# Two-layer spectral mixer and MLP on one core: third pair's sums on VectorE, half-width products around the last norm, matrix loads over 15 steps, more places for second weights

## The chip, the core and the metric

The kernel runs on one core of a Trainium2 chip. The engines are named as in the profile: PE (TensorE, with its weight loads as PEld), DVE (VectorE), ACT (ScalarE), POOL (GpSimd) and SP (SyncE), which here issues the program's DMA transfers. The metric is device time of one execution in microseconds (us), and of several executions the median.

## The reference

Four residual sublayers on x of shape (1, 2048, 576), all in float32: Fourier mixing, MLP, Fourier mixing, MLP. The MLP's weights are the same in both layers.

```python
def _A_ref(x, ...):                      # Fourier mixing
    a = einsum("bsd,ed->bse", x, dft_hid_re)
    b = einsum("bsd,ed->bse", x, dft_hid_im)
    return einsum("ts,bse->bte", dft_seq_re, a) - einsum("ts,bse->bte", dft_seq_im, b)

def _B_ref(x, w1, b1, w2, b2):           # w1: 576 x 4608, w2: 4608 x 576
    y = _layernorm(x, axis=-1)
    h = gelu(einsum("bsd,df->bsf", y, w1) + b1)
    return einsum("bsf,fd->bsd", h, w2) + b2

x = x + _A_ref(_layernorm(x)); x = x + _B_ref(_layernorm(x))
x = x + _A_ref(_layernorm(x)); x = x + _B_ref(_layernorm(x))
```

## The kernel before

**Number format.** A matmul operand is kept as two float32r parts, the rounded value (high) and the remainder (low). ACT writes the high part and DVE or POOL subtracts it to get the low one. A product is then three passes: high by high, high by low, low by high (`PASSES`).

**Seven products.** The big products are cut into 2 by 2 blocks and done with seven block products in place of eight; sums and differences of blocks are made before, and PE's results are combined by DVE, ACT and POOL after. `ORDER` is the order of the seven (1, 6, 2, 5, 7, 3, 4), `BANK` the PSUM bank of each: 1 and 2 share bank 0, 6 has bank 1, 5 and 3 share bank 2, 7 and 4 share bank 3. So product 2 can only start when product 1 has been copied out, 3 after 5 has been read, 4 after 7.

**Stages of a layer.** First the product along the sequence (`Sequence`). Then, for each half of the 2048 rows (first half, second half), eight row tiles of the product along the hidden dimension with the second layer norm (`hidden`), and the MLP on that half (`mlp`). The MLP goes over nine rounds `g`, each with two `inner` products (first weights, 512 columns) and the `outer` products of the round before (second weights): first the products 1, 6, 5, 3 (`OUTER[0]`), and after the second `inner` 7, 4, 2 (`OUTER[1]`). Each outer product is two steps of 12 matmuls, and the last round's outer products are 14 steps.

**What sets the order.** The program is a straight list; each engine runs its instructions in the order in which the Python code issues them, and waits on semaphores for data and for buffers. All DMA transfers stand in SP's one queue, in program order, so that a transfer that waits holds up the transfers behind it. Memory is two heaps, R (float32r) and A, in which places are taken and given back in program order.

**A tile end.** This happens four times, at the end of `hidden` (first and second layer, first and second half). The eight tiles make four pairs j = 0 to 3. For a pair, four blocks of the normalized rows are transposed (`turn_blocks`), then `turn_sums` writes the split of three of the blocks (`parts`, L846 on ACT and L194 on DVE) and makes four differences of 128 x 384 in place, and `turn_parts` writes the split of those four. For the last pair (j = 3) four differences of 128 x 288 are made on DVE in `norms` before the transposes, and `turn_y` transposes and splits its seven blocks in six pieces. The MLP's first product set is done in two halves: part 0 (256 columns, pairs 0 and 1) is a generator that yields after each of its seven products, and is advanced by `next(mlp)` here between the transposes; part 1 (pairs 2 and 3) follows and needs everything that `turn_parts(2)` and `turn_y(3)` write. Before the change the third pair (j = 2) has its differences on POOL during the last tile, and its parts, the last norm (L241) and the four differences of the last pair all come before the first copy (L1081) of the MLP's product 1.

**A hand-over.** This happens once a layer, from the MLP of the first half to `hidden` of the second half. During the last round's 14 outer steps `outer` advances a second generator, `steps()`, which loads the nine hidden matrices (R<-dh_parts, 576 KB each), the rows of the sequence product (R<-uv_mid) and x, and transposes the first tile. The matrices go to the place of `Y`, the MLP's input, which is given back at `g == NG`, when the last `inner` is over. Meanwhile the second weights of the last products need places too (`c2`): two from the start, and a third at `EXTRA_AT`. In the second layer `load_w` reads the prepared second weights (R<-w_parts) into a free place; in the first layer `make` prepares them (`hi` on ACT at L998, `lo` on DVE at L194), writes them out (w_parts<-R), and takes a place for each.

Of the kernel before, what the change touches and what calls it, by code (L numbers as in the profile page):

```python
# [153 lines left out]
def spectral_mixer(ctx: ExitStack, tc: tile.TileContext, x, dh, c0, cs, w1, b1, w2, b2, out):  # L154
# [487 lines left out]
    class Hidden:  # L642
# [42 lines left out]
        def steps(self):  # L685
            self.uvs = Slots(R, 2, 2 * D, Y_AT[0])
            self.X = A.place(X_AT[1], NT * DH)
            self.places = [R.place(Y_AT[0] + 4 * D + k * 2 * D, 2 * D) for k in range(KH)]

            def load_d(k):  # L690
                b = self.places[k].at
                self.load_d(k, Block(R, b, D), Block(R, b + D, D))

            self.load(0)
            load_d(0)
            yield
            self.load(1)
            load_d(1)
            for k in range(KH):
                yield  # L700
                if k + 2 < KH:
                    load_d(k + 2)
                self.high_d(k)
                if k:
                    self.low_d(k - 1)
            yield
            self.low_d(KH - 1)
            drain(self.turn(0, R.place(UT_AT[1][0], 2 * KH * P)))
            self.load_uv(2)
            yield  # L710
# [66 lines left out]
    def hidden(h, mlp):  # L777
# [18 lines left out]
        def norms(n):  # L796
# [10 lines left out]
            if n < NP - 1:  # L807
                add(nc.gpsimd, tile_x, tile_x, b2t(2, DH))
            else:
                b12, b22, b11, b21 = (v[:, k] for k in range(4))  # L810
                t1, t3, t2, t4 = (v[:, k] for k in range(4, 8))
                sub(nc.vector, t1, b12, b11)
                sub(nc.vector, t3, b22, b12)
                sub(nc.vector, t2, b22, t1)
                sub(nc.vector, t4, b21, t2)
# [34 lines left out]
        def turn_sums(j):  # L850
# [4 lines left out]
            g = nc.gpsimd  # L855
# [38 lines left out]
        for n in range(NP):  # L894
# [16 lines left out]
            for k in range(KH):  # L911
                if n == 0 and k == KH // 2:
                    drain(turn(1))
                if n >= 3 and n % 2 and k == 2:
                    turn_sums((n - 3) // 2)
# [11 lines left out]
            if n >= 3 and n % 2:  # L927
                turn_parts((n - 3) // 2)
            if n >= 2 and n % 2 == 0:
                turn_blocks(n // 2 - 1)  # L930


        drain(*ln)
        rests(3)
        y_steps = turn_y(3)
        for n in range(7):
            next(mlp)
            for _ in range((0, 0, 0, 1, 2, 1, 2)[n]):
                next(y_steps)
# [12 lines left out]
    def mlp(hid, store, first, after):  # L952
# [186 lines left out]
        def outer(g, i, side):  # L1139
            for jj in range(2):  # L1140
# [17 lines left out]
                if g == last:  # L1158
# [27 lines left out]
        for g in range(NG + 1):  # L1186
# [3 lines left out]
            if g == NG:  # L1190
                work(99)
                c1.close()
                hs.close()
                Y.free()
            for f in range(2):
                if g < NG:
                    for _ in inner(2 * g + f, None if g or f else 1):
                        pass
                if g:
# [86 lines left out]
```

## Time and profile before

| what | value |
|---|---|
| runs, us | 2773.51, 2768.78, 2773.53; median 2773.51 |
| profiled execution, us | 2768.23 |
| its span, first to last instruction, us | 2766.4 |
| granted PE clock, mean over the span | 0.992 |
| PE busy, us (share) | 2675.7 (97%) |
| DVE, ACT, POOL busy, us (share) | 1763.8 (64%), 1104.0 (40%), 804.9 (29%) |
| DMA, mean rate | 197 GB/s |

A row of the timeline reads: start in us, length in us, engine, line of the kernel, operation, what is written and read, shapes, count of merged instructions, and in square brackets the engine's idle time before it with what ended it. In a row of the windows stand the stretch, its length, the busy time of the engine with its count, the granted PE clock (1.00 is full speed), the busy share of the DMA engines and their GB/s.

### The profile page before, as it was taken

What the parts mean: (1) busy time and instruction counts of PE and PEld (TensorE: products, weight loads), DVE (VectorE), ACT (ScalarE), POOL (GpSimd) and SP (SyncE); (2) the same over time, 40 slices, a digit from 0 to 9 for tenths busy, and PEclk for the clock granted to TensorE, in tenths of its full rate; (3) what the DMA queues carried; (4) which work ended last, traced back from release to release, by engine and by line L of the source; (5) the groups of instructions that cost most, each with busy time, mean ns of one, the idle gap of its engine ahead of it and who ended that gap; (6) DMA issues with size and microseconds to landing.
All of it is one profiled execution on the core that took longest, in us unless ns stands there. A gap on an engine that the chain in (4) does not pass through costs nothing.

```text
span 2766.4 us, 45317 instructions
## 1 busy us (share of the span) xinstructions
PE 2675.7 (97%) x17488; PEld 2507.4 (91%) x17488; DVE 1763.8 (64%) x2566; ACT 1104.0 (40%) x1838; POOL 804.9 (29%) x762
## 2 busy tenths in 40 slices
PE   7999999999999999999989999999999999999998
PEld 7999998788888988989889999998999989898988
DVE  8788866777776465555577666555555545655555
ACT  6555545544443343333344333344333313433331
POOL 5222224544534432222251000042222224221222
PEclk9999999999999999999999999999999999999999
DMA  5666675777775646566553333526666563566664
GB/s 199 238 225 221 230 261 172 266 265 271 264 265 211 221 152 195 192 196 192 167 208 119 123 120 129 191 99 208 193 195 192 190 251 129 186 194 197 192 196 151
DMA packets 208711, 543.73 MB, mean 197 GB/s; under 512 B 21985, under 2 KB 56801, under 8 KB 208353
## 3 DMA queue, kind: packets, MB, share of 16 engines
q1 hardware_dynamic: 208496, 540.84, 57.8%
q8 instruction: 138, 2.26, 0.3%
q14 instruction: 77, 0.62, 0.1%
HBM read 428.69 MB, written 114.72 MB: 196 GB/s over the span
## 4 chain that ended last, share of the span: by engine, by line
PE 81%; DVE 6%; DMA 4%; issue 4%; POOL 2%; ACT 2%; SPq 0%; POOLq 0%; ACTq 0%; DVEq 0%
PE bank L201 80%; DVE R L194 3%; DMA R<-w_parts 2%; POOL A L194 2%; PE bank L764 1%; DVE A L191 1%; DMA A<-x_mid 1%; DMA A<-in_w 1%; DVE A L194 0%; DVE moments L231 0%; DVE bank L191 0%; DMA w_parts<-R 0%; ACT A L241 0%; SPq L188 0%; POOL R L194 0%
## 5 line engine op out<-in xcount | busy, mean ns | idle before, releaser
L201 PE MATMUL bank<-R 128*128 128x288 f32 (+2 forms) x16972 | 2629.7, 316 | 83.4 <-DVE A L191 26.3
L201 PEld LDWEIGHTS bank<-R 128*128 128x128 f32 x16972 | 2451.9, 190 | 250.5 <-DVE A L191 32.6
L191 DVE TENSOR_TENSOR A<-bank,A 128x576 f32<-128x576 f32 (+3 forms) x808 | 566.9, 710 | 565.2 <-PE bank L201 484.0
L194 POOL TENSOR_TENSOR R<-A,R 128x512 fp32r<-128x512 f32 x288 | 374.8, 1312 | 978.8 <-ACT R L1114 955.7
L194 DVE TENSOR_TENSOR R<-A,R 128x1024 fp32r<-128x1024 f32 (+10 forms) x521 | 494.0, 972 | 82.1 <-ACT R L846 37.1
L191 POOL TENSOR_TENSOR A<-A 128x576 f32<-128x576 f32 (+2 forms) x102 | 135.8, 1333 | 641.9 <-ACT A L592 350.5
L1054 ACT ACTIVATE bank<-bank,b1t 128x512 f32<-128x512 f32 (+1 forms) x224 | 144.8, 647 | 374.5 <-DVE bank L191 252.8
L1114 ACT ACTIVATE R<-A 128x512 fp32r<-128x512 f32 x288 | 176.1, 629 | 275.0 <-DVE A L194 118.3
L194 POOL TENSOR_TENSOR A<-A 128x384 f32<-128x384 f32 (+2 forms) x170 | 211.4, 1250 | 180.5 <-DVE R L194 101.9
L554 ACT ACTIVATE R<-A 128x1024 fp32r<-128x1024 f32 x196 | 204.0, 1054 | 134.5 <-DVE A L194 105.2
L191 DVE TENSOR_TENSOR bank<-bank,A 128x512 f32<-128x512 f32 (+1 forms) x228 | 152.1, 669 | 153.3 <-PE bank L201 153.0
L194 DVE TENSOR_TENSOR R<-bank,R 128x512 fp32r<-128x512 f32 x336 | 210.3, 640 | 61.5 <-ACT R L197 51.7
L1114 ACT ACTIVATE R<-bank 128x512 fp32r<-128x512 f32 x216 | 120.8, 596 | 32.5 <-PE bank L201 32.5
L194 DVE TENSOR_TENSOR A<-A 128x1024 f32<-128x1024 f32 (+2 forms) x116 | 127.7, 1106 | 3.1
L1081 ACT ACTIVATE A<-bank 128x512 f32<-128x512 f32 (+1 forms) x76 | 43.7, 574 | 211.7 <-PE bank L201 208.7
L194 DVE TENSOR_TENSOR A<-bank,A 128x512 f32<-128x512 f32 x144 | 98.0, 680 | 0.0
L197 ACT ACTIVATE R<-bank 128x512 fp32r<-128x512 f32 (+1 forms) x112 | 50.4, 491 | 101.8 <-PE bank L764 84.9
L241 ACT ACTIVATE A<-A,moments 128x576 f32<-128x576 f32 x64 | 53.7, 863 | 56.2 <-POOL moments L237 30.2
L594 DVE SCALAR_TENSOR_TENSOR A<-A 128x288 f32<-128x288 f32 x28 | 18.4, 657 | 89.6 <-POOL A L191 89.6
L1054 ACT ACTIVATE A<-bank,b1t 128x512 f32<-128x512 f32 (+1 forms) x76 | 50.4, 663 | 56.7 <-DVE bank L191 56.7
L846 ACT ACTIVATE R<-A 128x768 fp32r<-128x768 f32 (+2 forms) x36 | 32.8, 947 | 73.9 <-POOL A L194 73.9
L268 ACT ACTIVATE R<-A,power,middle 128x128 fp32r<-128x128 f32 x126 | 60.8, 482 | 0.0
(58 smaller groups left out, 632.5 us busy)
## 6 DMA issues: line engine op xcount, KB each, us to landing
R<-w_parts SPq DMA_DIRECT2D x504, 320.0 KB, 3.3
R<-w_parts SPq DMA_DIRECT2D x189, 576.0 KB, 3.6
A<-in_cs SPq DMA_DIRECT2D x112, 512.0 KB, 4.1
w_parts<-R SPq DMA_DIRECT2D x126, 320.0 KB, 4.0
w_parts<-R SPq DMA_DIRECT2D x63, 576.0 KB, 3.9
uv_mid<-A SPq DMA_DIRECT2D x32, 576.0 KB, 2.8
A<-in_w SPq DMA_DIRECT2D x72, 192.0 KB, 3.6
R<-dh_parts SPq DMA_DIRECT2D x23, 576.0 KB, 10.6
```

The source lines that it names most:

```text
L191: engine.tensor_tensor(dst, a, b, op=op)
L194: engine.tensor_tensor(dst, a, b, op=OP.subtract)
L197: nc.scalar.activation(hi, src, AF.Copy)
L201: nc.tensor.matmul(o, a, b, start=start, stop=stop, skip_group_check=True)
L241: nc.scalar.activation(dst, src, AF.Identity, bias=mv[:, 4:5], scale=mv[:, 3:4])
L268: nc.scalar.activation(t[:, 2], src[:, 1], AF.Identity, bias=power[:, 2:3], scale=middle)
L554: nc.scalar.activation(self.cells[t, i](2, NP, P)[:, 0], self.source(t, i), AF.Copy)
L764: nc.tensor.transpose(at, v[:, k], ident)
L846: nc.scalar.activation(y[:, i, 0:3, at], x, AF.Copy)
L1054: nc.scalar.activation(dst, src, AF.Gelu_apprx_tanh, bias=bias(f))
L1081: nc.scalar.activation(up, o, AF.Copy)
L1114: nc.scalar.activation(H[q, k](2, TC)[:, 0], src, AF.Copy)
```

## The change

- In `steps()` the first rows (`load_uv(0)`) and the nine matrices come first, one matrix a step; the place `X` and the loads of x follow, and six steps later the transposes of the first tile. The code that split the matrices there is gone; `made` is always true where `steps()` is used, so that it did nothing.
- `outer` advances that generator also in the six steps of the round before the last products (`g == last - 1 and side == 0`), in the first half only, so 20 steps are there for it. For this `c1` and `Y` are given back right after the last `inner`, one group of outer products earlier.
- In the first half `c2` gets a fourth place at R 0 when that is free (`len(c2.idle) < 4`), and two more at the place of `c1` after the last `inner`.
- At a tile end the third pair's `turn_sums(2)` is issued at the end of the seventh tile in place of inside the last, its four differences are on DVE, and four half-width products are issued around the last norm: two, then `turn_parts(2)` and the norm, then two, then the four differences of the last pair (a `yield` in `norms` parts them from the norm).

```diff
         def steps(self):
             self.uvs = Slots(R, 2, 2 * D, Y_AT[0])
-            self.X = A.place(X_AT[1], NT * DH)
             self.places = [R.place(Y_AT[0] + 4 * D + k * 2 * D, 2 * D) for k in range(KH)]
-
-            def load_d(k):
+            self.load_uv(0)
+            for k in range(KH):
                 b = self.places[k].at
                 self.load_d(k, Block(R, b, D), Block(R, b + D, D))
-
+                yield
+                if k == 2:
+                    self.load_uv(1)
+            self.X = A.place(X_AT[1], NT * DH)
             self.load(0)
-            load_d(0)
             yield
             self.load(1)
-            load_d(1)
-            for k in range(KH):
+            for _ in range(6):
                 yield
-                if k + 2 < KH:
-                    load_d(k + 2)
-                self.high_d(k)
-                if k:
-                    self.low_d(k - 1)
-            yield
-            self.low_d(KH - 1)
             drain(self.turn(0, R.place(UT_AT[1][0], 2 * KH * P)))
...
             if n < NP - 1:
                 add(nc.gpsimd, tile_x, tile_x, b2t(2, DH))
             else:
+                yield
                 b12, b22, b11, b21 = (v[:, k] for k in range(4))
...
             parts(j, slice(0, 1), slice(2, 3))
-            g = nc.gpsimd
+            g = nc.gpsimd if j < 2 else nc.vector
             sub(g, b11, b12, b11)
...
-                if n >= 3 and n % 2 and k == 2:
+                if n in (3, 5) and k == 2:
                     turn_sums((n - 3) // 2)
...
-            if n >= 3 and n % 2:
+            if n in (3, 5):
                 turn_parts((n - 3) // 2)
             if n >= 2 and n % 2 == 0:
                 turn_blocks(n // 2 - 1)
-        drain(*ln)
+            if n == NP - 2:
+                turn_sums(2)
+        for _ in range(2):
+            next(mlp)
+        turn_parts(2)
+        next(g)
+        for _ in range(2):
+            next(mlp)
+        drain(g)
         rests(3)
         y_steps = turn_y(3)
-        for n in range(7):
+        for n in (1, 2, 3):
             next(mlp)
-            for _ in range((0, 0, 0, 1, 2, 1, 2)[n]):
+            for _ in range(n):
                 next(y_steps)
...
-                if g == last:
+                if g == last or half == 0 and g == last - 1 and side == 0:
                     next(after, None)
...
             if g == NG:
                 work(99)
-                c1.close()
                 hs.close()
-                Y.free()
+            if half == 0 and len(c2.idle) < 4:
+                more = R.place(0, 4 * DH)
+                if more:
+                    c2.idle.append(more)
             for f in range(2):
                 if g < NG:
                     for _ in inner(2 * g + f, None if g or f else 1):
                         pass
+                if g == last and f:
+                    c1.close()
+                    Y.free()
+                    if half == 0:
+                        c2.idle += [R.place(C1_AT[0] + k * 4 * DH, 4 * DH) for k in range(2)]
```

How this moves instructions is seen in the order in which they stand on an engine. The first place is DVE's queue at a tile end. In these rows 128x2x288 is the sum of the last tile's product with x, BN_STATS to L219 its moments, 128x4x2x128 with 32x4x128 the low parts of the third pair, 128x288 x4 the last pair's differences, and 128x256 a sum for a half-width product. Before:

```order
L191 TENSOR_TENSOR A<-bank,A 128x2x288
L216 BN_STATS moments<-A 128x6 x2
L217 BN_AGGR moments<-moments 128x2
L219 TENSOR_SCALAR moments<-moments 128x1
L194 TENSOR_TENSOR R<-A,R 128x4x2x128
L194 TENSOR_TENSOR R<-A,R 32x4x128
L194 TENSOR_TENSOR A<-A 128x288 x4
L191 TENSOR_TENSOR A<-bank,A 128x256 x2
L194 TENSOR_TENSOR R<-bank,R 128x2x2x128
```

The last row is the low part of the first transposed piece of the last pair. DVE's queue at the same place with the change:

```order
L194 TENSOR_TENSOR A<-A 128x384 x4
L191 TENSOR_TENSOR A<-bank,A 128x2x288
L216 BN_STATS moments<-A 128x6 x2
L217 BN_AGGR moments<-moments 128x2
L219 TENSOR_SCALAR moments<-moments 128x1
L191 TENSOR_TENSOR A<-bank,A 128x256
L194 TENSOR_TENSOR R<-A,R 128x4x2x128
L194 TENSOR_TENSOR R<-A,R 32x4x128
L191 TENSOR_TENSOR A<-bank,A 128x256
L194 TENSOR_TENSOR A<-A 128x288 x4
L191 TENSOR_TENSOR bank<-bank,A 128x256
L194 TENSOR_TENSOR R<-bank,R 128x2x2x128
```

Four sums of 128 x 384 have come in ahead of the last tile's sum, and three sums for half-width products stand ahead of the first transposed piece, with the third pair's low parts and the last pair's differences between them.

The second place is SP's queue at the hand-over of the second layer. R<-w_parts of 128x1152 is one product's second weights, R<-dh_parts one hidden matrix, R<-uv_mid one tile's rows, A<-x_mid x. Before, from the last weights of the rounds on:

```order
L188 DMA R<-w_parts 128x1152 x3
L188 DMA R<-uv_mid 128x1152
L188 DMA A<-x_mid 128x2x288
L188 DMA R<-dh_parts 128x1152
L188 DMA R<-uv_mid 128x1152
L188 DMA A<-x_mid 128x2x288
L188 DMA R<-dh_parts 128x1152
L188 DMA R<-w_parts 128x1152
L188 DMA R<-dh_parts 128x1152 x2
L188 DMA R<-w_parts 128x1152
L188 DMA R<-dh_parts 128x1152 x2
L188 DMA R<-w_parts 128x1152
```

Behind the last of these rows stand two more matrices, one more product's weights and the last matrix. SP's queue at the same place with the change:

```order
L188 DMA R<-w_parts 128x1152
L188 DMA R<-uv_mid 128x1152
L188 DMA R<-dh_parts 128x1152
L188 DMA R<-w_parts 128x1152
L188 DMA R<-dh_parts 128x1152
L188 DMA R<-w_parts 128x1152
L188 DMA R<-dh_parts 128x1152
L188 DMA R<-uv_mid 128x1152
L188 DMA R<-dh_parts 128x1152
L188 DMA R<-w_parts 128x1152
L188 DMA R<-dh_parts 128x1152 x2
L188 DMA R<-w_parts 128x1152
```

Behind it stand two matrices, the weights of the last product, one matrix, and then x. The weights of the last six products and the matrices are now dealt out one by one from the first of the 20 steps on, with x behind them all.

## The prediction, written before the changed kernel ran

> **What bounds the kernel now.** I read the page first, then PE's own timeline for its idle time, then all engines around the places that the change touches.
>
> ```profile
> PE 2675.7 (97%) x17488; PEld 2507.4 (91%) x17488; DVE 1763.8 (64%) x2566; ACT 1104.0 (40%) x1838; POOL 804.9 (29%) x762
> ```
>
> PE is busy for 97% of the span, and the change adds and removes no matmul. So it can only win from PE's idle time, 2766.4 - 2675.7 = 90.7 us in all, and from matmuls that ran slowly behind it. PE's idle time is one of many short waits, which the change doesn't touch, and of few long ones. Two kinds of long ones stand where the change is: the tile end, four times, and the hand-over, twice.
>
> The tile end of the second layer's first half, from the timeline of all engines:
>
> ```profile
> 1842.55 7.43 PE L201 MATMUL bank<-R 128*128 128x288 f32 x54
> 1843.40 0.58 ACT L839 ACTIVATE A<-bank 96x512 f32<-96x512 f32 x1
> 1845.55 1.24 ACT L846 ACTIVATE R<-A 128x768 fp32r<-128x768 f32 x2
> 1846.41 2.46 DVE L194 TENSOR_TENSOR R<-A,R 128x512 fp32r<-128x512 f32 x4 [2.84 <-ACT R L846]
> 1849.04 4.24 POOL L194 TENSOR_TENSOR A<-A 128x384 f32<-128x384 f32 x4 [1.88 <-DVE R L194]
> 1850.02 0.76 DVE L191 TENSOR_TENSOR A<-bank,A 128x576 f32<-128x576 f32 x1 [1.15 <-PE bank L201]
> 1850.83 1.94 PE L201 MATMUL bank<-R 128*128 128x256 f32 x14 [0.85 <-DVE A L191]
> 1853.32 1.48 ACT L846 ACTIVATE R<-A 128x1536 fp32r<-128x1536 f32 x1 [6.53 <-POOL A L194]
> 1854.71 0.85 ACT L241 ACTIVATE A<-A,moments 128x576 f32<-128x576 f32 x1
> 1854.83 1.92 DVE L194 TENSOR_TENSOR R<-A,R 128x1024 fp32r<-128x1024 f32 x2 [2.77 <-ACT R L846]
> 1855.47 0.36 ACT L1081 ACTIVATE A<-bank 128x256 f32<-128x256 f32 x1
> 1855.88 1.95 PE L201 MATMUL bank<-R 128*128 128x256 f32 x14 [3.11 <-ACT A L1081]
> 1856.78 1.69 DVE L194 TENSOR_TENSOR A<-A 128x288 f32<-128x288 f32 x4
> 1859.25 0.68 DVE L194 TENSOR_TENSOR R<-bank,R 128x512 fp32r<-128x512 f32 x1
> 1859.85 0.42 DVE L191 TENSOR_TENSOR bank<-bank,A 128x256 f32<-128x256 f32 x1
> 1860.20 1.29 DVE L194 TENSOR_TENSOR R<-bank,R 128x512 fp32r<-128x512 f32 x2
> 1861.07 0.39 ACT L197 ACTIVATE R<-bank 128x256 fp32r<-128x256 f32 x1
> 1861.87 0.47 ACT L1054 ACTIVATE A<-bank,b1t 128x256 f32<-128x256 f32 x1 [0.42 <-DVE bank L191]
> 1862.96 1.16 DVE L194 TENSOR_TENSOR R<-bank,R 32x512 fp32r<-32x512 f32 x2 [0.47 <-ACT R L888]
> 1863.71 6.58 PE L201 MATMUL bank<-R 96*128 96x256 f32 x48 [0.37 <-DVE R L194]
> ```
>
> PE ends the last tile at 1849.98, does products 1 and 6 at half width, and then stands for 3.11 us. The releaser is the copy of product 1 (L1081). That copy took 0.36 us but stood in ACT's queue behind the norm (L241) and the third pair's parts (L846), and those had waited 6.53 us for POOL's four differences. So POOL's 4.24 us are on the path. The stage ends at 1863.71, when part 1's first 96-row matmul can go: 13.73 us after the last tile. The other three, from PE's timeline:
>
> ```profile
> 442.83 7.43 PE L201 MATMUL bank<-R 128*128 128x288 f32 x54
> 456.18 3.36 PE L201 MATMUL bank<-R 128*128 128x256 f32 x14 [3.13 <-ACT A L1081]
> 466.54 10.26 PE L201 MATMUL bank<-R 96*128 96x256 f32 x64 [0.37 <-DVE R L194]
> 973.64 7.43 PE L201 MATMUL bank<-R 128*128 128x288 f32 x54
> 996.34 385.85 PE L201 MATMUL bank<-R 96*128 96x256 f32 x2268 [0.37 <-DVE R L194]
> 2335.18 7.43 PE L201 MATMUL bank<-R 128*128 128x288 f32 x54
> 2357.88 401.56 PE L201 MATMUL bank<-R 96*128 96x256 f32 x2388 [0.37 <-DVE R L194]
> ```
>
> From the end of the 54 to the 96-row matmul: 16.28, 15.27 and 15.27 us. The same work takes up to 2.55 us more than in the first stage. The windows say why: the granted clock (the second number from the count on).
>
> ```profile
> 456.00:458.00 2.00, 1.82 (x8) 0.50 0.00 0
> 1856.00:1858.00 2.00, 2.00 (x18) 1.00 0.00 0
> ...
> 903.00:905.00 2.00, 2.00 (x10) 0.50 1.03 424
> 2258.00:2260.00 2.00, 2.00 (x10) 0.50 1.01 410
> 2246.00:2270.00 24.00, 19.36 (x134) 0.93 0.98 393
> ```
>
> After the wait PE ran at half clock at 456 and at full clock at 1856: 8 matmuls in one window and 18 in the other, and 3.36 us for the same 14 that took 1.95. A long wait is thus paid twice in most places. The rows at 903 and 2258 are the hand-overs, with the same thing:
>
> ```profile
> 900.08 0.68 ACT L998 ACTIVATE R<-A 128x576 fp32r<-128x576 f32 x1 [6.80 <-DMA w_parts<-R]
> 902.36 4.90 PE L201 MATMUL bank<-R 128*128 128x288 f32 x24 [5.55 <-DVE A L191]
> ```
>
> In the first layer the last product's second weights (L998) waited 6.80 us for a place whose old content was still being written out. Their low part on DVE stands ahead of the sums that free PE's banks, and so PE stood 5.55 us. In the second layer:
>
> ```profile
> 2214.96 37.60 PE L201 MATMUL bank<-R 128*128 128x288 f32 x241
> 2256.74 8.11 PE L201 MATMUL bank<-R 128*128 128x288 f32 x48 [4.17 <-DMA R<-w_parts]
> 2265.32 3.44 PE L201 MATMUL bank<-R 128*128 128x288 f32 x24 [0.47 <-DMA R<-w_parts]
> R<-w_parts SPq DMA_DIRECT2D x189, 576.0 KB, 3.6
> ```
>
> PE waited 4.17 us for second weights. A load of them takes 3.6 us in the median, but here they stood in the DMA queue among the hidden matrices, and DMA was busy for 0.98 of the time from 2246 to 2270.
>
> **The change, part by part.**
>
> *VectorE's sums.* Four differences of 128 x 384 leave POOL (4.24 us) for DVE. No row shows them there; the four of 128 x 288 take 1.69, so by size at most 1.69 x 384/288 = 2.25 (bounds: 1.69, and POOL's own 4.24). They also come earlier: the parts before them no longer stand behind the seventh tile's norm, so ACT starts them when L839 ends (1843.98), DVE follows 0.86 later as it does in the rows (1844.84), is done after 2.46 (1847.3) and with the sums at 1849.55. The last tile's sum starts at 1850.02. They fit with 0.5 to spare and cost nothing while that holds; at POOL's 4.24 they would push that sum, and all behind it, by 1.5 us. POOL loses work that nobody else waits for.
>
> *Half-width products around the norm.* I walk the stage in us from the last tile's end, with the rows' lengths. PE starts product 1 at 0.85 as before (the bank is free only after the tile's sum) and ends product 6 at 2.8. ACT's copy comes right behind product 1, at about 2.1 to 2.45, so the 3.11 us wait goes and PE runs on through 2, 5 and 7. But all the rest now queues on DVE. ACT: parts 1.48 (to 3.9), norm 0.85 (4.7). DVE: sum for product 6 (0.42, to 3.3), low parts 1.92 from 3.9 (5.8), sum for 5 (6.2), differences 1.69 (7.9), sum for 7 (8.3), piece 1 (0.68, 9.0), sum for 3 (9.4), pieces 2 and 3 (1.29, 10.7), sum for 4 (11.1). Then a step back and forth: ACT's gelu 0.47 and copy 0.39 (12.0), DVE's piece 4 (as wide as the sums, 0.42, 12.4) and the first of the two 32-row pieces (half of 1.16, 13.0). PE goes on at 13.0 us. It has been done with all else by about 11, so a new wait of about 2 us stands there. Four times 13.0 are 52.0 against 60.55 (13.73 + 16.28 + 15.27 + 15.27): **8.5 us** less. With full clock before and after, the saving would be 0.7 a stage only; the other 5.6 come from matmuls that are no longer slowed. Bounds for one stage: 12.2, if DVE's instructions overlap at their ends as some rows do, and 14.7, if the sums cost POOL's price.
>
> The new wait of 2 us may itself halve the clock. In the rows it was halved after 3.13 us, and not after 3.11. If 2 us were enough, part 1's matmuls would lose about what the second layer's second half lost beside its first, 1.54 us, four times: 6.2.
>
> [...]
>
> *More places.* In the first layer the fourth place opens only in the last round (the places from R 0 are the first weights' staging until those are made), but there six places are then free when seven products are prepared. L998 waits for no write any more, DVE's queue isn't held, and the 5.55 us go. With them goes the half clock behind: 24 matmuls took 4.90, and at the 7.43/54 = 0.138 of the rows above they take 3.3. Together **7.2 us**. I see no price on the other side: what is written is read again only in the next half.
>
> *Matrix loads over 15 steps.* Second layer: 12 of 20 steps were done when PE stopped at 2252.56, so step 1 began at 2252.56 - 12 x 12 x 0.138 = 2232.7. With the change 17 transfers of 576 KB follow from there, at 393 GB/s 1.5 us each, the first landing 3.6 us after its issue. The weights of the last three products are the 10th, 13th and 16th: 2249.8, 2254.3, 2258.8. They are wanted at steps 15, 17 and 19: 2255.9, 2259.2, 2262.5. All are in time, by 3.7 us at the least, and the last matrix is there before the first tile. So 4.17 + 0.47 and the slow matmuls (8.11 - 48 x 0.138 = 1.5) go: **6.1 us**. Loading x at steps 10 and 11 in place of 7 and 8, and transposing the first tile one step earlier, moves nothing that PE waits for. In the first layer the same transfers go ahead of the writes, which nobody waits for then.
>
> The sum: 8.5 + 7.2 + 6.1 = 21.8 us. It is made against the profiled execution, whose span is 2766.4 and time 2768.2; the median of the runs shown is 2773.5, so that this one is 5.3 below it, as much as one halved stage here or there. I take the middle, 2770.9, as the base: 2770.9 - 21.8 = **2749**.
>
> **The rivals.**
>
> *The tile end gives nothing* (18%). VectorE takes the place of POOL: its queue is 0.7 us from being as late as the old wait in the one stage with full clock, and the new wait halves the clock. For it: the walk's last 10 us are DVE and ACT alone. Against it: three of four stages had the slow clock already. Then 7.2 + 6.1 remain: 2757.6.
>
> *The hand-overs give nothing* (10%): the weights are as late as before because the matrices still take the queue, or the places stay unused. For it: DMA had no time left there. Against it: by the program's order the last weights are now asked for eight to ten steps ahead of their use, before four. Then 8.5 remain: 2762.4.
>
> *Even* (6%): both in part, within 0.2% of before, 2770.
>
> *Slower* (6%): the matrices, now dealt out between the weights, hold these up more than before. Its place is the second layer's hand-over, its price 15 times the growth of one transfer beyond 1.75 us, where the 16th is just in time. It decides against the whole change when it eats 21.8 us and 5.5 more: the old loss of 6.1 is in those 21.8, so 27.3/15 = 1.8 over, 3.6 us a transfer or 164 GB/s. The row says 393, with other rows at 410 and 424; the mean over the span is lower because less was asked. Then about 2778.
>
> **How the numbers follow.** My forecast has 60%, the others 18, 10, 6 and 6. Runs here spread by some 0.2% (5.5 us), and that is what a measurement can tell from no change. Faster than 2768: 60 + 18 + 7 of the 10 = 85%; within 0.2%: 9%; slower: 6%. The range: down to 2738, if the stages come to 12.2 (3.2 less), the base is the profiled one (2.7 less) and other slow stretches happen to fall away; up to 2766, with both middle rivals inside.
>
> **What would show it.** Right: no wait of 3.1 us behind the first 14 half-width matmuls, 35 of them in a row, and about 13.0 us from the last tile's 54 to the 96-row matmul, with DVE busy almost throughout and a wait of about 2 us at the end. The four 128 x 384 on DVE, near 0.56 us each, ending ahead of the last tile's sum. No wait of L998 for w_parts<-R, and no wait of PE for R<-w_parts before the transposes of the second half; R<-dh_parts issued from step 1 on. Wrong: 14 us or more in the stages, a clock of 0.50 right behind them, or weights that land after their step.

## The result, and the profile after

| | before | with the change |
|---|---|---|
| median of 4 runs, us | 2771.15 (2768.08 to 2773.53) | 2744.36 (2743.38 to 2747.72) |
| ratio to before, 95% interval | | 0.9906 (0.9889 to 0.9923) |
| span of the profiled execution, us | 2766.4 | 2743.1 |
| four tile ends, us | 16.28, 15.27, 13.73, 15.27 | 12.10, 12.10, 12.11, 12.11 |
| hand-over, first layer, us | 38.71 | 32.77 |
| first half's MLP and hand-over, second layer, us | 413.27 | 407.13 |

Times go from the end of the last tile's 54 matmuls to part 1's first 96-row matmul (tile end), from the lone matmul of 128 x 288 some 20 to 30 us ahead of the first nine transposes to the second nine transposes (first layer), and from part 1's first 96-row matmul to the second nine transposes (second layer). The change is faster by 0.94%, and the forecast of 2749.0 is 4.6 us too high. Of the spans' 23.3 us, 12.1 come from the tile ends, 5.9 from the first hand-over and 6.1 from the second; the other stretches together lose 0.8.

The first part of the page after:

```profile
PE 2668.6 (97%) x17488; PEld 2497.0 (91%) x17488; DVE 1774.5 (65%) x2582; ACT 1102.5 (40%) x1838; POOL 789.5 (29%) x746
```

PE has as many matmuls as before and is busy for 7.1 us less: in the clock's record 41.6 us of the span of before ran at half clock, and 19.4 of the span of after (mean granted clock 0.992 and 0.996); its idle time fell by 16.2 us, from 90.7 to 74.5.

A tile end after, from the timeline of all engines:

```profile
442.18 7.43 PE L201 MATMUL bank<-R 128*128 128x288 f32 x54
...
444.52 3.00 DVE L194 TENSOR_TENSOR R<-A,R 128x512 fp32r<-128x512 f32 x4 [1.33 <-ACT R L840]
...
445.74 1.63 POOL L191 TENSOR_TENSOR A<-A 128x576 f32<-128x576 f32 x1 [1.37 <-ACT A L241]
447.65 2.34 DVE L194 TENSOR_TENSOR A<-A 128x384 f32<-128x384 f32 x4
449.91 0.75 DVE L191 TENSOR_TENSOR A<-bank,A 128x576 f32<-128x576 f32 x1
...
450.71 4.47 PE L201 MATMUL bank<-R 128*128 128x256 f32 x35 [1.11 <-DVE A L191]
...
451.86 0.38 ACT L1083 ACTIVATE A<-bank 128x256 f32<-128x256 f32 x1 [6.19 <-PE bank L201]
...
453.51 0.86 ACT L241 ACTIVATE A<-A,moments 128x576 f32<-128x576 f32 x1
453.64 1.92 DVE L194 TENSOR_TENSOR R<-A,R 128x1024 fp32r<-128x1024 f32 x2 [0.47 <-ACT R L840]
...
455.94 1.68 DVE L194 TENSOR_TENSOR A<-A 128x288 f32<-128x288 f32 x4
...
459.32 0.49 ACT L1056 ACTIVATE A<-bank,b1t 128x256 f32<-128x256 f32 x1
459.68 0.40 ACT L197 ACTIVATE R<-bank 128x256 fp32r<-128x256 f32 x1
...
460.20 0.42 DVE L191 TENSOR_TENSOR bank<-bank,A 128x256 f32<-128x256 f32 x1
...
460.53 1.60 DVE L194 TENSOR_TENSOR R<-bank,R 128x256 fp32r<-128x256 f32 x3
461.71 7.01 PE L201 MATMUL bank<-R 96*128 96x256 f32 x50 [0.73 <-DVE R L194]
```

The copy of product 1 (L1083) now comes 1.15 us after product 1 begins, and 35 half-width matmuls stand in one row without the 3.1 us wait. Three things differ from the forecast's walk. The third pair's low parts took 3.00 us, not 2.46, so that the tile's sum (449.91) stands right behind the differences and PE's first wait is 1.11 us, not 0.85. The last gelu and its copy (459.32, 459.68) run ahead of the last sum (460.20), not behind it. And the wait at the end is 0.73 us, not 2.

The windows of the same tile end:

```profile
450.00:462.00 12.00, 10.10 (x78) 9.24 (x79) 10.41 (x22) 7.70 (x13) 4.30 (x8) 1.00 0.18 53
```

The granted clock (the number behind the five engines) is 1.00 throughout. Before, it was 0.50 at 456. In the trace's record of the clock, no tile end has a half-clock stretch now; before, three of the four had.

The two hand-overs after, from PE's timeline:

```profile
880.74 11.37 PE L201 MATMUL bank<-R 128*128 128x288 f32 x84 [0.20 <-DVE A L191]
893.12 1.85 PE L201 MATMUL bank<-R 128*128 128x288 f32 x12 [1.00 <-DVE A L191]
...
2214.69 30.99 PE L201 MATMUL bank<-R 96*128 96x512 f32 x219
2245.52 1.14 PE L757 MATMUL bank<-ident,R 128*128 128x128 f32 x9
```

In the first layer 1.00 us is left of 5.55. In the second layer PE runs on from the 96-row matmuls to the transposes: neither wait for second weights is left.

### The profile page after: what moved, and what is told of

It reads as the page before. It is cut to its first block, busy times and chain, and to the rows that moved or that the text cites. A ratio compares the mean times of both kernels' runs of the same rounds, so it can differ in the third digit from the quotient of the medians.

```text
span 2743.1 us, 45319 instructions
## 1 busy us (share of the span) xinstructions
PE 2668.6 (97%) x17488; PEld 2497.0 (91%) x17488; DVE 1774.5 (65%) x2582; ACT 1102.5 (40%) x1838; POOL 789.5 (29%) x746
## 5 line engine op out<-in xcount | busy, mean ns | idle before, releaser
L194 POOL TENSOR_TENSOR A<-A 128x384 f32<-128x384 f32 (+2 forms) x154 | 195.5, 1277 | 168.2 <-DVE R L194 96.4
L1083 ACT ACTIVATE A<-bank 128x512 f32<-128x512 f32 (+1 forms) x76 | 43.8, 576 | 237.8 <-PE bank L201 235.2
L194 DVE TENSOR_TENSOR A<-A 128x1024 f32<-128x1024 f32 (+3 forms) x132 | 136.6, 1040 | 4.0
L267 ACT ACTIVATE R<-A 128x256 fp32r<-128x256 f32 x126 | 51.3, 407 | 12.2 <-DMA A<-in_w 8.3
```

The costliest lines, as they stand in the source:

```text
L194: engine.tensor_tensor(dst, a, b, op=OP.subtract)
L267: nc.scalar.activation(t[:, 1:4:2], src[:, 0:3:2], AF.Copy)
L1083: nc.scalar.activation(up, o, AF.Copy)
```

## The experiments

Each kernel is the one before or the changed one with the edit shown. Where a median stands, the kernel was timed in several rounds beside the kernel before; where one time stands, it ran once.

**1. The tile end's edits alone** (`t_only`): of the diff above, only the hunks in `norms`, `turn_sums`, `turn_parts` and the loop around them.

```diff
+                yield
...
-            g = nc.gpsimd
+            g = nc.gpsimd if j < 2 else nc.vector
...
+            if n == NP - 2:
+                turn_sums(2)
...
+        for _ in range(2):
+            next(mlp)
+        turn_parts(2)
...
```

> The kernel before with the tile end of the change alone (four half-width products around the norm, third pair's sums on VectorE). Theory A, the two halves of the change are independent and add up: the four tile ends take 12.1 us each, as in the changed kernel (before 16.3, 15.3, 13.7, 15.3), the hand-overs stay at 39.5 us in the first layer (end of the 157 matmuls to the second set of transposes) and keep PE's wait for second weights in the second; time about 12 us under before, 2759 against 2771. Rival B, the tile end's gain is given back further on (the MLP's first rounds wait for weights): stages 12.1, but the time within 4 us of before.

Measured: 2759.99 us beside 2769.08, ratio 0.9962 (0.9950 to 0.9975). Its tile ends take 12.11, 12.12, 12.10 and 12.11 us, and the waits of the hand-overs remain, from PE's timeline:

```profile
898.73 5.96 PE L201 MATMUL bank<-R 128*128 128x288 f32 x24 [4.67 <-DVE A L191]
...
2250.65 12.19 PE L201 MATMUL bank<-R 128*128 128x288 f32 x72 [4.30 <-DMA R<-w_parts]
```

The tile ends are a saving of their own of about 9 us. Their 12.1 us don't all arrive: the first hand-over took 39.94 us here beside 38.71, as the 24 matmuls behind the wait lost more to the clock (5.96 us, before 4.90). In the profiled execution 8.2 us of the span are left; the rest is spread over other stretches, at most 1.1 us in each, and no run shows why.

**2. The hand-over's edits alone** (`h_only`): the hunks in `steps()`, `outer` and `c2`, without the tile end's.

```diff
-                if g == last:
+                if g == last or half == 0 and g == last - 1 and side == 0:
                     next(after, None)
...
+                        c2.idle += [R.place(C1_AT[0] + k * 4 * DH, 4 * DH) for k in range(2)]
```

> The kernel before with the hand-over of the change alone (loads over 15 steps and more places). Theory A: 33.5 us in the first layer's hand-over in place of 39.5, and no wait of PE for second weights in the second layer, together 12 us: 2759. The four tile ends have before's instructions; by the clock theory each takes 13.7 us at full clock and up to 2.6 more where the clock is granted at 0.50 behind the wait of 3.1 us, and which ones are slow differs from the profile of before. Rival: the tile ends take the same 16.3, 15.3, 13.7, 15.3 again, so that something of the stage itself makes the difference.

Measured: 2757.84 beside 2769.08, ratio 0.9957 (0.9943 to 0.9971). The second hand-over is as short as with the whole change (406.64); the first takes 33.84 us beside 32.77, with its half-clock stretch at another place (96 matmuls in 14.49 us, 13.2 at 0.138 each; experiment 9). The tile ends, whose program is that of before, took 15.16, 15.27, 16.41 and 13.70 us: another order of long and short than before (16.28, 15.27, 13.73, 15.27). So these differences don't belong to a place in the program. The second 14 half-width matmuls of the third and the fourth, from PE's timeline:

```profile
1848.42 3.36 PE L201 MATMUL bank<-R 128*128 128x256 f32 x14 [3.13 <-ACT A L1074]
```

```profile
2337.09 1.93 PE L201 MATMUL bank<-R 128*128 128x256 f32 x14 [3.11 <-ACT A L1074]
```

The same wait is followed by 3.36 us in the one and by 1.93 in the other. The medians of the two halves add up to 20.3 us, beside 26.8 for the whole change, and 24.3 when that ran once more (experiment 10). Each of these has an interval of some 4 us to either side, so the runs neither show nor exclude that the halves add up.

**3. More places alone** (`places_only`): the early release of `c1` and `Y`, the fourth place and the two at `C1_AT`; `steps()` and its calls as before.

```diff
+            if half == 0 and len(c2.idle) < 4:
+                more = R.place(0, 4 * DH)
+                if more:
+                    c2.idle.append(more)
...
+                    if half == 0:
+                        c2.idle += [R.place(C1_AT[0] + k * 4 * DH, 4 * DH) for k in range(2)]
```

> The kernel before with the places for second weights alone (fourth place, two more after the last inner product, with the earlier giving back that this needs); the matrices are loaded over the last 14 steps as before. Theory S, as the prediction has it (places carry the first layer, the loads over more steps carry the second): first layer's hand-over 33 to 34 us, but the second layer still waits 4 to 5 us for R<-w_parts; time 6 us under before. Theory P (places carry both, because the last weights are asked for eight to ten steps ahead): no wait for R<-w_parts in the second layer either; time 11 to 12 us under before, 2760.

Measured: 2761.24 beside 2769.08, ratio 0.9968 (0.9957 to 0.9979). PE's timeline, and one row of SP's:

```profile
897.35 3.41 PE L201 MATMUL bank<-R 128*128 128x288 f32 x24 [1.00 <-DVE A L191]
...
915.27 1.20 PE L764 MATMUL bank<-ident,R 128*128 128x128 f32 x9 [1.20 <-DMA R<-uv_mid]
...
925.54 2.05 PE L764 MATMUL bank<-ident,R 128*128 128x128 f32 x9 [1.88 <-DMA R<-uv_mid]
...
2214.76 43.82 PE L201 MATMUL bank<-R 128*128 128x288 f32 x291
...
2243.63 0.42 SPq L188 DMA_DIRECT2D R<-w_parts  x1
```

The places take away the waits of both hand-overs but for 1.00 us: 291 matmuls in one row at 2214.76 in the second, and 406.56 us for its MLP and hand-over, as with the whole change. There the last second weights are issued at 2243.63, ahead of seven of the nine matrices; before, the last were issued at 2261.71, behind eight of them. In the first layer the price shows: the matrices are late, the rows (R<-uv_mid) stand behind them, and PE waits for these 1.20 and 1.88 us in the first tiles of the second half, with a half-clock stretch behind (14 matmuls in 2.95 us at 927.25, 1.9 at 0.138 each). From the second nine transposes to the end of the last tile this layer takes 70.49 us beside 65.58 before, so that of the 6.0 us won in its hand-over (32.67 from 38.71) 4.9 are lost again.

**4. The loads over 15 steps alone** (`loads_only`): `steps()` and its earlier calls, with the release that they need, but no more places.

> The kernel before with the matrix loads over more steps alone, three places for second weights as before. Theory S: no wait for R<-w_parts in the second layer, the first layer as before (39.5 us in the hand-over); time 6 us under before. Theory P: the last weights are still asked for only four steps ahead, now behind matrices from the first step on, so PE waits for R<-w_parts 4 us or more in the second layer; in the first layer the writes find the queue emptier and the wait of 5.5 us may shrink; time 0 to 6 us under before.

Measured: 2761.84 beside 2769.08, ratio 0.9972 (0.9962 to 0.9982). PE's timeline:

```profile
880.20 14.48 PE L201 MATMUL bank<-R 128*128 128x288 f32 x96 [1.97 <-DVE A L191]
895.68 1.82 PE L201 MATMUL bank<-R 128*128 128x288 f32 x12 [1.00 <-DVE A L191]
...
2238.97 3.44 PE L201 MATMUL bank<-R 128*128 128x288 f32 x24 [1.05 <-DMA R<-w_parts]
```

The loads, too, remove the first layer's wait nearly as far (33.85 us from 38.71), since six of the nine matrices are now issued ahead of the last writes that free places (ACT's longest wait for such a write at L991 is 2.21 us, before 6.80). In the second layer they leave a wait of 1.05 us for second weights and two of 0.83 for DVE, and take 410.48 us: 2.8 us less than before, where the places alone won 6.7. Alone, the two are worth 7.8 and 7.2 us by the medians, together (`h_only`) 11.2: in the first layer they remove the same wait. From part 1's first 96-row matmul to the end of the second half's last tile, in one profiled execution each, the places win 1.3 us in the first layer and 6.7 in the second, the loads 4.6 and 2.8, both together 5.4 and 6.6.

**5. The sums on POOL, all else as changed** (`pool_sums`).

```diff
-            g = nc.gpsimd if j < 2 else nc.vector
+            g = nc.gpsimd
```

> The changed kernel with the third pair's four differences on POOL again, at their new place in the program. Theory O, the order of the products around the norm is what shortens the tile end, and where the differences run is next to nothing: they end on POOL about 2.2 us after the last tile, before ACT comes to the third pair's parts, and the last tile's sum on VectorE is no longer pushed (PE's first wait 0.85 in place of 1.11); stages 11.8 to 12.2. Theory V, VectorE's sums are needed: the third pair's parts wait for POOL again, stages 13 us or more.

Measured: 2744.99 us in one run, and all four tile ends 11.85 us, from the timeline of all engines:

```profile
446.77 4.28 POOL L194 TENSOR_TENSOR A<-A 128x384 f32<-128x384 f32 x4 [2.19 <-PE bank L201]
...
450.68 4.46 PE L201 MATMUL bank<-R 128*128 128x256 f32 x35 [0.85 <-DVE A L191]
```

POOL's four take 4.28 us and end at 451.05, in time for the parts that ACT writes only after product 1's copy. The tile end is 0.25 us shorter than with the sums on DVE.

**6. The sums on DVE and issued early, the products as before** (`dve_sums_only`).

```diff
-            g = nc.gpsimd
+            g = nc.gpsimd if j < 2 else nc.vector
...
+            if n == NP - 2:
+                turn_sums(2)
```

> The kernel before with the third pair's differences on VectorE at the end of the seventh tile, alone; products, parts and norm in before's order. Theory O: the copy of product 1 still stands behind the norm, which ends at about 4.2 us, so that PE waits about 1.8 us in place of 3.1, and a stage takes about 12.4 at full clock. As 1.8 us can still halve the clock in some phases, one or two of the four may be slower. Theory V: stages as in the changed kernel, 12.1, with no wait of PE above 1.2.

Measured: 2771.95 us in one run beside 2768.98, tile ends 15.07, 15.07, 15.11 and 13.53 us. A step of the norm in the first, from the timeline of all engines, and the second 14 matmuls of the first and the last, from PE's:

```profile
453.46 1.47 POOL L222 TENSOR_TENSOR moments<-moments,power 128x1 f32<-128x1 f32 x1 [4.65 <-DVE moments L219]
...
456.76 2.70 PE L201 MATMUL bank<-R 128*128 128x256 f32 x14 [2.67 <-ACT A L1082]
...
2353.11 1.94 PE L201 MATMUL bank<-R 128*128 128x256 f32 x14 [2.66 <-ACT A L1082]
```

The sums alone gain little: at full clock the last stage takes 13.53 us, where the unchanged one takes 13.70 to 13.74 (experiments 2 to 4). PE still waits 2.67 us for product 1's copy, which stands behind the parts and the norm in ACT's queue. Theory O's 1.8 us were too few because the norm came late: POOL's first step for it (L222) took 1.47 us beside DVE's low parts, 0.55 in the kernel before. Of the tile end's two edits the order of the products is the one that pays.

**7. POOL's add of the seventh tile after the stage** (`late_add`).

```diff
-            if n < NP - 1:
+            if n < NP - 2:
                 add(nc.gpsimd, tile_x, tile_x, b2t(2, DH))
-            else:
+            if n == NP - 1:
...
-        tile_x = xv[:, :, order[NP - 1]]
-        add(nc.gpsimd, tile_x, tile_x, b2t(2, DH))
+        for n in (NP - 2, NP - 1):
+            tile_x = xv[:, :, order[n]]
+            add(nc.gpsimd, tile_x, tile_x, b2t(2, DH))
```

> The changed kernel with POOL's addition of b2 to the seventh tile moved behind the stage. In the changed kernel VectorE's low parts of the third pair took 3.00 us in place of 2.46 and its four differences 2.34, while POOL did that addition. Theory C, the two engines slow each other when both work from memory to memory: 2.46 and about 2.1, PE's first wait 0.85 in place of 1.11, stages 11.85. Rival: 3.00 and 2.34 stay, because of what stands ahead on ACT or VectorE.

Measured: 2744.21 us in one run, all four tile ends 11.86 us. The smallest of the low parts' four instructions, from the groups by line and shape, in the changed kernel and then in this one (busy us, mean ns, idle us before):

```profile
L194 DVE TENSOR_TENSOR R<-A,R 32x128 fp32r<-32x128 f32 x1 | 1.4, 1419 | 0.0
```

```profile
L194 DVE TENSOR_TENSOR R<-A,R 32x128 fp32r<-32x128 f32 x1 | 0.3, 282 | 0.0
```

This one makes the whole difference: 0.28 us alone and 1.42 beside POOL's add. The four together are 1.86 us without the add and 3.00 with it, the sums 2.34 either way, and PE's first wait is back at 0.85. Theory C's cause was right (POOL's add), and its 2.46 for the parts too long: in the kernel before, too, POOL's add ran beside them, and the one of 128x512 took 1.30 us there, 0.69 here.

**8. Product 1 in a bank that is free earlier** (`bank3`).

```diff
-                o, ring = pp[0], [2, 3] * 3
+                o, ring = pp[3], [2, 3] * 3
```

> The changed kernel with the last tile's product in the fourth pair of PSUM banks in place of the first, so that the half-width product 1 doesn't wait for VectorE's sum of the last tile. If that wait of 1.11 us is on the path (the third pair's parts on ACT stand behind the copy of product 1, and VectorE behind them): stages 11.0 to 11.3, four times about 1 us, time about 2740 against 2744 for the changed kernel. If VectorE's own queue sets the end whenever product 1 comes: stages 12.1 as they are.

Measured: 2743.45 (2741.10 to 2745.01) beside 2768.98, ratio 0.9899 (0.9883 to 0.9916). Tile ends 11.51, 11.36, 11.36 and 11.36 us, from the timeline of all engines:

```profile
442.55 11.62 PE L201 MATMUL bank<-R 128*128 128x288 f32 x89
...
450.85 0.38 ACT L1083 ACTIVATE A<-bank 128x256 f32<-128x256 f32 x1 [4.82 <-PE bank L201]
...
452.64 1.92 DVE L194 TENSOR_TENSOR R<-A,R 128x1024 fp32r<-128x1024 f32 x2
453.02 0.89 POOL L223 TENSOR_TENSOR moments<-moments 128x1 f32<-128x1 f32 x1
454.00 0.62 POOL L224 TENSOR_TENSOR moments<-power,moments 128x1 f32<-128x1 f32 x1
...
455.57 0.66 PE L870 MATMUL bank<-ident,A 128*128 128x128 f32 x4 [1.40 <-ACT A L241]
```

The last tile and the first five products (54 and 35 matmuls, of 288 and 256 columns) now are one row of 89, and the first wait is gone. Some of it comes back as a new wait of 1.40 us for the norm: DVE's low parts now fall on POOL's two small steps for the norm, which take 0.89 and 0.62 us in place of 0.20 and 0.19.

**9. The last low part two steps later in the first hand-over** (`lo2_later`).

```diff
-                    advance(6 + 15 * f)
-                    at[0] = 7 + 15 * f
+                    to = 15 if f and g == NG else 6 + 15 * f
+                    advance(to)
+                    at[0] = to + 1
```

> The change, with the low part of the very last second weights (product 2) issued two outer steps later in the first layer's hand-over, so that only one low part of 128x576 stands ahead of the sums that free PE's banks. Theory S (the two stacked low parts hold DVE and so PE): the 1.00 us wait of PE at 893 falls below 0.3, and the first layer's hand-over is about 0.7 to 1 us shorter. Rival (the POOL add beside them slows DVE, or the bank is late for another reason): the wait stays at 0.8 or more.

Measured: 2743.60 us in one run. The place in the changed kernel, from the timeline of all engines, and then PE's timeline with the edit:

```profile
889.65 2.65 DVE L194 TENSOR_TENSOR R<-A,R 128x576 fp32r<-128x576 f32 x2
889.81 1.88 POOL L191 TENSOR_TENSOR A<-A 128x576 f32<-128x576 f32 x1 [0.15 <-DVE A L191]
892.23 1.41 DVE L191 TENSOR_TENSOR A<-bank,A 128x576 f32<-128x576 f32 x2
...
893.12 1.85 PE L201 MATMUL bank<-R 128*128 128x288 f32 x12 [1.00 <-DVE A L191]
```

```profile
873.60 3.34 PE L201 MATMUL bank<-R 128*128 128x288 f32 x23 [0.99 <-DVE R L194]
878.87 16.11 PE L201 MATMUL bank<-R 128*128 128x288 f32 x108 [1.93 <-DVE A L191]
```

The 1.00 us wait is gone: 108 matmuls in one row. Yet the hand-over is only 0.16 us shorter (32.61 from 32.77), because this run has its half-clock stretch at another place: the 23 matmuls at 873.60 ran at full clock, which only turned 0.4 us of waiting for DVE into 1.93, and the 108 took 1.2 us more than at 0.138 each. The wait falls as theory S said, and the time that it is worth is seen between runs with the half clock at the same place: 33.84 us in `h_only`, whose hand-over is the change's, to 32.61 here, and 32.77 with the change to 31.49 in the next run. It is 1.2 to 1.3 us.

**10. Edits 7, 8 and 9 together** (`all_three`), and **the change once more** (`change_again`) on the same chip.

> The change with product 1 in a fourth bank, POOL's add of the seventh tile after the stage, and the low part of the last second weights two steps later. Bank theory with free DVE: the stages fall from 12.10 to 11.0 to 11.3 us, below the 11.36 of the bank alone, and 0.7 to 1 us goes in the first hand-over: about 2740. If the stage is held by POOL's small steps of the last norm alone, the later add brings nothing beside the bank: 11.36 and about 2741.

> The change itself once more, beside the combined version on the same chip: 2744, 1% below the kernel before, stages of 12.1 us.

Measured, beside 2769.52 for the kernel before: the combined version 2740.99 us, ratio 0.9901 (0.9885 to 0.9918); the change 2745.26, ratio 0.9912 (0.9897 to 0.9926), with tile ends of 12.10 and 12.11 us. The combined version's first hand-over takes 31.49 us, 1.28 less than the change's 32.77, with the half clock where the change has it. Its tile ends stay at 11.51 and three times 11.36, so that the later add brings nothing beside the other bank. POOL's steps in it, by line and shape:

```profile
L223 POOL TENSOR_TENSOR moments<-moments 128x1 f32<-128x1 f32 x1 | 1.2, 1152 | 0.1
L224 POOL TENSOR_TENSOR moments<-power,moments 128x1 f32<-128x1 f32 x1 | 0.6, 617 | 0.1
```

By the rows the tile end is now held by POOL's small steps beside DVE's low parts, as the second expectation had it; no run takes these steps away from there. It is the fastest of the kernels here: 4.3 us below the change by the medians of one chip, though the two intervals against the kernel before overlap.

## Why the prediction came out as it did, point by point

**What bounds.** Right: the time came from PE's idle time and from matmuls at half clock, at the two kinds of places named, and hardly anywhere else.

**The sums cost nothing while they fit with 0.5 to spare.** This step failed. The walk took 2.46 us for the low parts ahead of them, from the trace of before, and got 3.00, because POOL's add of the seventh tile ran against them; DVE's sums themselves took 2.34, near the 2.25 of the estimate. The spare time was gone and 0.26 us of PE's first wait came on top, four times (experiments 5 and 7 take them away). Nor was there anything to win by the move: the text had POOL's 4.24 us on the path, which holds only while product 1's copy stands behind the parts. Once the copy comes first, POOL has time enough.

**The walk to 13.0 us.** The mechanism was right, the term of 8.5 us too small: 12.1 were measured. Counted from the last tile's end at 449.61, the walk has the third pair's low parts done at 5.8, the differences at 7.9, the first piece at 9.0, pieces 2 and 3 at 10.7 and the last sum at 11.1; the rows of after give 5.95, 8.0, 8.9, 10.7 and 11.0. Then it put a gelu and a copy on ACT (0.47 + 0.39) behind the last sum. In the rows this gelu is over before that sum starts, since it reads product 3's bank and not product 4's. So 0.9 us a stage were counted that aren't on the path: some 3.5 in four stages, nearly the whole difference between 8.5 and 12.1. Of the 12.1, 6.5 are the shorter stage at full clock (13.73 to 12.10), and 5.6 half clock that is gone; the latter depends on how many stages the run of before had slow.

**The new wait of 2 us and the half clock behind it.** It is 0.73 us, so the case that it halves the clock did not arise. That the 8.5 us count no half clock behind a wait of 2 us was the author's estimate; in the kernel before half clock begins at 499.41, behind a wait of 1.81 us that ends at 498.56. In experiment 6 a wait of 2.66 or 2.67 us was followed by half clock in three stages and by full clock in one. So half clock came behind waits well below 3.11 us, and the text's line between 3.11 and 3.13 us is none: in the kernel before, the wait of 3.11 us ahead of 986.97 was followed by half clock as well. The last section shows what parts the two cases.

**More places 7.2 us, matrix loads 6.1 us.** The sum of 13.3 was near (12.1 measured); the attribution failed, so that the near sum is partly luck. The text gave the first layer to the places and the second to the loads. The mechanism of the first holds: with the places ACT waits for no write any more (L998 in `places_only`, L1000 in the change). But "no price on the other side" does not: alone they lose 4.9 of 6.0 us again to late rows, a price that the change escapes only by its earlier loads. In the second layer it is the places that carry all 6.7 us alone; the loads alone win 2.8. The steps that failed are this price, put at nothing, and the walk of the second layer's transfers, which took the places as given and asked only how the queue is filled. The first layer's 7.2 came to 5.9 mainly because of the 1.00 us wait that the text did not see: two low parts on DVE, one of them held up by POOL's add (experiment 9).

**The sum.** 21.8 us were forecast and 23.3 measured in the spans: 3.6 too little in the tile ends, 1.3 too much in the first hand-over, and the other stretches of the program differ by at most 1.3 us, with both signs. By the medians the change wins 26.8 us: 3.5 more than by the spans, as the profiled execution of before lay 2.9 us below its median and that of after 0.5 above. The rivals: the tile ends gave most, so did not give nothing; the hand-overs gave 12.1; the matrices did not hold up the weights, and PE waits for none of these in the second layer's hand-over.

**The tile ends that differ.** The text put 2.55 us between equal stages down to the clock. `h_only`, `places_only` and `loads_only` bear it out: with the program of the tile end unchanged, its twelve samples lie between 13.70 and 16.41 us and trade places. The clock record confirms it: of the 16 samples with those of before, the six without half clock take 13.70 to 13.74 us, the seven with one stretch of 3.41 us 15.16 to 15.30, and the three with one of 6.83 us 16.27 to 16.41. So "before" is not one number: the 16 samples of the unchanged form have a mean of 14.9, and the profiled one with 60.55 for four was at the long end (as `h_only`; 58.0 in `loads_only`). The eight samples with the change, here and in `t_only`, all lie between 12.10 and 12.12.

## What to carry to other kernels

Where an engine waits for one short copy that stands in a queue behind long work, move the copy, not the work: here the order of four products paid and a faster engine for the sums did not (2.34 us on DVE, 4.28 on POOL, and the tile end 0.25 us longer with DVE). When a walk along the queues is made, take each instruction's operands bank by bank, since one wrong dependency at the end costs every stage (here 0.9 us). Measure edits apart before crediting them: two of them can remove the same wait, and the durations taken from a profile can already be longer because of another engine (here 2.46 us for low parts that took 1.86 without POOL's add beside them).

## What the runs showed of the hardware

**DVE and POOL beside each other.** In the changed kernel POOL's add begins at 445.74 and is over at 447.37. DVE's instructions in that time, from DVE's timeline in that stretch:

```profile
446.10 1.42 DVE L194 TENSOR_TENSOR R<-A,R 32x128 fp32r<-32x128 f32 x1
```

Alone it takes 0.28 us (experiment 7), and here it ends at 447.52, just after POOL's add. The other way round, in `all_three`:

```profile
452.68 1.23 DVE L194 TENSOR_TENSOR R<-A,R 128x1024 fp32r<-128x1024 f32 x1 [0.21 <-ACT R L840]
```

POOL's 128x1 step of 0.19 us begins at 452.81 beside it and takes 1.15, to 453.96, just after DVE's end at 453.91. In these rows the small instruction took 1.42 us for 0.28 and 1.15 for 0.19, and ended 0.15 and 0.05 us after the other engine's large one, as if it had waited for the whole of it. A sum on DVE that reads a bank was not held: in the changed kernel one of 128x576 takes 0.76 us at 888.98, beside POOL's add of the same size from 888.23 to 889.66, and 0.76 at 887.39, where POOL stands idle. What makes the difference is not shown.

**Half clock after waits shorter than 3.1 us, and not always.** In experiment 6 the same wait, from the windows right behind it in the first and the last stage (clock third from the end):

```profile
458.00:460.00 2.00, 2.00 (x12) 2.00 (x11) 0.92 (x3) 0.45 (x2) 1.69 (x4) 0.50 0.00 0
2354.00:2356.00 2.00, 2.00 (x19) 2.00 (x19) 1.23 (x4) 0.92 (x2) 1.27 (x4) 1.00 0.00 0
```

A wait of 2.67 us was followed by 0.50, one of 2.66 us by 1.00. What parts the two is seen in the clock records of the 13 kept traces. In each, the half-clock stretches last 3.41 us or a multiple of it, apart from the one at the program's end, and they start whole multiples of 3.41 us apart, on one grid. (In the kernel before they start at 455.04, 499.41, 878.29, 898.77 and so on, and the first four last 6.83, 3.41, 3.41 and 6.83 us.) With that grid laid over PE's timeline, there are 10306 periods at full clock. All 51 in which PE stood for 1.81 us or more in sum are followed by half clock, and none of the 10242 in which it stood for less than 1.75; of the 13 between, nine are. The kernel before and the changed one have 1588 of these periods: all 11 with 1.81 us or more are followed by half clock, and none of the 1575 with less than 1.75. By these counts it is how much of the waiting falls into one period that parts the two cases, not the wait's length alone. The first stage's wait, 454.09 to 456.76, lies with 2.58 us in the period that ends at 457.59. The last one's, 2350.45 to 2353.11, is parted by the grid at 2351.99, into 1.54 and 1.12 us. No run shifts a wait on purpose to try it, and PE's idle time is known only as well as the modelled ends of its matmuls. The price is about 1.5 us for a stage with one such stretch (15.07 us beside 13.53 in experiment 6), and waits of 1.4 us and less in the tile ends were not followed by one.
